# Scratch of q and k in two parts a row instead of three, and the stacks read in two transfers each

## The chip, the cores and the metric

The kernel runs on one core of one Trainium2 chip. The time is device microseconds of one execution of the whole program on that core; the kernel before took 1964.72 us, the median of three runs (1963.83, 1964.72 and 1965.18 us). TensorE is called PE here, VectorE DVE, ScalarE ACT, GpSimd POOL, and SyncE SP. SP computes nothing: it issues nearly all the transfers, in the order of the program, and waits in that order too.

## The reference: what is computed

The kernel adds three things for 2048 tokens of width 512: the input, an attention block with 32 heads of width 16, and a gated MLP that mixes tokens.

```python
xn = _layernorm(x)
# attention
qkv = (xn @ wqkv).reshape(B, S, 3, H, Dh)        # S 2048, H 32, Dh 16
p = softmax(einsum("bhqd,bhkd->bhqk", q, k) * Dh ** -0.5)
a = einsum("bhqk,bhkd->bhqd", p, v).reshape(B, S, D) @ wo
# gated MLP
z = gelu(einsum("bsd,df->bsf", xn, w_in)); z1 = z[..., :896]
z2 = _layernorm(z[..., 896:])
g = einsum("ts,bsf->btf", w_sp, z2) + b_sp
out = x + a + einsum("bsf,fd->bsd", z1 * g, w_out)
```

## The kernel before

**Numbers in two parts.** Products of float32 values are made from a high part, which TensorE's fast float32 format holds exactly, and a low part, the rest. An ordinary product is three matmuls, high by high, low by high and high by low (`mm3`, L161 to L164). For the scores, where a head is only 16 wide, the three are stacked in the rows of one matmul: a head's stack has KS = 48 rows, three for each of the 16 features. A feature's three rows hold high, low, high on the side of q and high, high, low on the side of k, so that one matmul over 48 rows gives all three products.

**Where the stacks come from.** q and k are made for 8 heads at a time (m = 0 to 3) and for 512 tokens at a time (g = 0 to 3), with feature and head across the 128 partitions (`qk_group`, L287). `qk_split` (L305) makes the two parts in a buffer `qkhl`, 128 partitions x 2 x 512, of which there are three (`hilo`, L146): ACT writes the high part, then DVE (m = 0) or POOL (m = 1 to 3) writes the low part. `qk_store` (L278) stores them to the scratch `qscr[m]` or `kscr[m]` in HBM, [128, 3, 2048]: one transfer of 512 KB for both parts and one of 256 KB that stores the high part a second time. The buffer is free for the next split when both have landed. `load_stacks` (L598) reads a head's 48 rows from there into the SBUF tiles `qst` and `kst`, where they lie in partitions 0 to 47 for the first head of a pair and 64 to 111 for the second: for pair 0 in blocks of 512 tokens, in the prologue, and for each later pair in four transfers of 48 rows of 8 KB.

**The order of the work.** The program is written out once, and each engine runs its share of it in that order. A prologue normalises x, makes q and k of the first 8 heads, all of v, and the stacks of pair 0. Then a loop runs over 16 pairs of heads x 4 blocks of queries x 16 tiles of keys. A tile of scores is two matmuls (`st`, L903), one exp on ACT, and the product with v (`o`, L877). The largest score of each row is found 27 tiles ahead: the same scores are made the other way round (`mx`, L630), DVE reduces them (`mm`, L638), and the results go through HBM (`mscr`) into rows 48 and 49 of the stack `qst`. The score tiles and the maxima share three PSUM buffers. A planner fills the rest of TensorE's time with the other matmuls, a few in each half step of the loop: `qk` of the remaining heads, then the MLP, then the product with `wo`. Transfers that need not go at once are put off by some half steps (`later`, L125; in the loop `store` puts a store off by one, L134), and the weights that the filler needs are fetched and split on POOL by `prepare` (L191) in the same manner. The planner decides all this when the program is written, from estimates; on the chip the engines then only wait for each other by semaphores. A transfer's completion is told by one of eight semaphores in turn, so that each transfer also waits for the one eight before it.

**What the change touches.** The scratch tiles (L80 and L81), `qk_store`, `qk_split`, and `load_stacks`. In the order of SP lie around them the reloads of the normalised input (`xnT`), the row maxima (`mscr`), the chunks of the attention output (`escr`), and the weights (`w_`, `wsp_`).

Of the kernel before, what the change touches and what calls it, by code (L numbers as in the profile page):

```python
# [8 lines left out]
F32 = mybir.dt.float32  # L9
F32R = mybir.dt.float32r  # L10
AF = mybir.ActivationFunctionType
# [5 lines left out]
P = 128  # L17
S = 2048
D = 512
H = 32  # L20
DH = 16
# [6 lines left out]
KS = 3 * DH  # L28
# [11 lines left out]
def fused_block(ctx, tc, x, wqkv, wo, w_in, w_spT, b_sp, w_out, out):  # L40
    nc = tc.nc
    cp = ctx.enter_context(tc.tile_pool(name="const", bufs=1))
    dr = ctx.enter_context(tc.tile_pool(name="scratch", bufs=1, space=DRAM))
# [11 lines left out]
    def act(out, in_, func, n, **kw):  # L55
        load["A"] += 0.16 + n / 1400.0
        return nc.scalar.activation(out, in_, func, **kw)  # L57

    def dve(n, rate=1):
        load["D"] += 0.065 + n / (960.0 * rate)  # L60
        return nc.vector
# [15 lines left out]
    qst = [cp.tile([P, S], F32R, name=f"qst{a}") for a in range(2)]  # L77
    kst = [cp.tile([P, S], F32R, name=f"kst{a}") for a in range(2)]

    qscr = [dr.tile([P, 3, S], F32, name=f"qscr{m}") for m in range(4)]  # L80
    kscr = [dr.tile([P, 3, S], F32, name=f"kscr{m}") for m in range(4)]  # L81
    xscr = [[dr.tile([P, 2, 512], F32, name=f"xscr{g}_{c}") for c in range(ND)] for g in range(NG)]
    z2scr = dr.tile([P, NF, 2, NT, P], F32, name="z2scr")
    z1scr = [dr.tile([P, NG, 512], F32, name=f"z1scr{f}") for f in range(NF)]
# [12 lines left out]
    def raw(t):  # L97
        return t.bitcast(F32) if t.dtype == F32R else t

    def move(dst, src):  # L100
        nc.sync.dma_start(raw(dst), raw(src))
# [10 lines left out]
    def clock():  # L112
        return HALF * now[0]

    def gps(us):
        pool[0] = max(pool[0], clock()) + us
        return nc.gpsimd

    def pool_done():
        t = pool[0]  # L120
        yield
        while clock() < t:
            yield

    def later(k, fn, *args):  # L125
        late.append((now[0] + k, fn, args))
# [19 lines left out]
    def hilo(nm):  # L146
        return big.tile([P, 2, 512], F32R, tag="hilo", name=nm, bufs=3)
# [127 lines left out]
                one(c)  # L275


    def qk_store(scr, order, hl, sl, first=False):  # L278
        put = move if first else store
        r = 1 if order[0] == order[1] else 0  # L280
        put(scr[:, r:r + 2, sl], hl)
        put(scr[:, 2 - 2 * r, sl], hl[:, 0, :])

    def qk_weights(m, a):
        return f"wqk{m}_{a}", wqkv[:, a * D + m * P: a * D + (m + 1) * P], D, ND

    def qk_group(m, g, w, tags=("d",)):  # L287
        for a in range(2):
            if now[0] < -2 and m:
                tags = ("d", "o")  # L290
            acc = dpsum(f"qk{m}_{a}_{g}", tags[a % len(tags)], ND)
            for c in range(ND):
                t = xnT[g, c]
                mm3(acc, w[a][:, 0, c * P:(c + 1) * P], w[a][:, 1, c * P:(c + 1) * P], t[:, 0, :], t[:, 1, :], c == 0, c == ND - 1)
                yield 650 + 0.5 * (c == ND - 1)
            if m == 0:
                run(qk_split(m, g, a, acc))
                yield 0
                continue
            raw_ = t512(f"qr{m}_{a}_{g}")  # L300
            act(raw_, acc, AF.Copy, 512)
            side.append(qk_split(m, g, a, raw_))
            yield 0

    def qk_split(m, g, a, src):  # L305
        hl = hilo(f"qkhl{m}_{a}_{g}")
        act(hl[:, 0, :], src, AF.Copy, 512)
        yield
        if m:
            gps(1.3).tensor_sub(hl[:, 1, :], src, hl[:, 0, :].bitcast(F32))  # L310
            yield from pool_done()
        else:
            dve(512).tensor_sub(hl[:, 1, :], src, hl[:, 0, :].bitcast(F32))
        qk_store((qscr, kscr)[a][m], ((0, 1, 0), (0, 0, 1))[a], hl, slice(g * 512, (g + 1) * 512), m == 0)
        yield

    def qk_prepare():
# [280 lines left out]
    def load_stacks(p, cols=slice(0, S)):  # L598
        m, r = p // 4, (p % 4) * 2
        q, k = qst[p % 2], kst[p % 2]  # L600
        sl = [slice((r + j) * DH, (r + j + 1) * DH) for j in range(2)]
        for j in range(2):
            for i, (t, scr) in enumerate(((q, qscr), (k, kscr))):
                args = t[64 * j:64 * j + KS, cols], scr[m][sl[j], :, cols]
                if p and 2 * j + i:
                    later(2 * j + i, move, *args)
                else:
                    move(*args)

# [203 lines left out]
    with tc.manual_schedule(engines=engines):  # L815
# [6 lines left out]
        for c in range(ND):  # L822
            t = (qst, kst)[c // 2][1].rearrange("p (b a f) -> p b a f", b=2, a=2)[:, c % 2]
# [12 lines left out]
        for g in range(NG):  # L836
            for y in qk_group(0, g, w0, ("d", "o")):
                if y == 0 and g == 0:
                    next(norm, 0)
            load_stacks(0, slice(g * 512, (g + 1) * 512))  # L840
            if g == NG - 2:
                for a in range(2):
                    wq[1, a] = begin(*qk_weights(1, a))
            if g == NG - 1:
                for a in range(2):
                    wq[1, a] = end(wq[1, a])
            for t in range(4 * g, 4 * g + 4):
                next(norm, 0)
                if t % 4 == 2:
                    if g + 1 < NG:  # L850
                        turn_x(g + 1)
                    if g + 2 < NG:
                        norm = norm_x(g + 2)
                v_tile(t, wv)
# [50 lines left out]
        order = [(p, c, kt) for p in range(NP) for c in range(NG) for kt in range(NT)]  # L905
# [37 lines left out]
        for half in range(-2 * LEAD // 3, 2 * (N // 3 + 4)):  # L943
# [5 lines left out]
            for n in ns:  # L949
                if n == 16:  # L950
                    init_rows(1)
                if n % 64 == 14 and n // 64 + 1 < NP:
                    load_stacks(n // 64 + 1)
# [99 lines left out]
```

## Time and profile before

| | |
|---|---|
| median of three runs | 1964.72 us |
| the profiled execution: time, span | 1965.23 us, 1963.1 us |
| PE busy | 1933.9 us, 99% of the span |
| DVE, ACT, POOL busy | 1372.9, 1231.7, 720.9 us |
| granted TensorE clock, mean | 0.997 |
| transfers of the SP queue | 282.08 MB, 49.4% of the 16 DMA engines' time |
| HBM written | 101.97 MB |

The profile tells for each engine when it was busy, and for each idle stretch what ended it. A wait is written "engine line <- who: us in total, times, longest". The chain is the work that ended last, followed back from the end, so a step that is not in it costs nothing. A stage of the span is read from a table by windows: the busy time of each engine in that stretch, the granted clock, the share of time in which the DMA engines were busy, and the GB/s moved.

### The profile page before, as it was taken

To read this page: it belongs to the slowest core of one execution; us is meant where nothing else is said; L and a number is where in the kernel's file an instruction comes from. 1 tells how busy PE (TensorE), PEld (TensorE's weight loads), DVE (VectorE), ACT (ScalarE), POOL (GpSimd) and SP (SyncE) were. 2 spreads that over 40 slices of the span, in tenths; PEclk is the share of its full clock that TensorE was granted. 3 is DMA by queue.
4 is the path that set the end of the run, shared out by engine and by line. 5 is a ranking of instruction groups with operands and counts; after the bars stand their busy time and mean duration, and the time that the engine had idled before them with its cause. 6 is when DMAs were issued, how large, how long until landed. Compare 5 with 4: busy or idle time off the path is not lost.

```text
span 1963.1 us, 32545 instructions
## 1 busy us (share of the span) xinstructions
PE 1933.9 (99%) x12544; PEld 1047.0 (53%) x12544; DVE 1372.9 (70%) x1562; ACT 1231.7 (63%) x1402; POOL 720.9 (37%) x787
## 2 busy tenths in 40 slices
PE   7999999999999999999999999999999999999998
PEld 6765555555555555555555555555555555555543
DVE  5256777777777677777777777777777777777872
ACT  4336778888777665656666665665566655556664
POOL 2234368789776931026122531017112300002100
PEclk9999999999999999999999999999999999999999
DMA  9586444363535645365545744346364645355323
GB/s 327 204 292 200 139 107 122 108 176 111 154 117 159 187 123 140 91 162 159 151 138 154 211 129 125 108 126 204 105 163 135 176 142 145 106 152 154 105 73 113
DMA packets 234195, 294.20 MB, mean 150 GB/s; under 512 B 34536, under 2 KB 134520, under 8 KB 231160
## 3 DMA queue, kind: packets, MB, share of 16 engines
q1 hardware_dynamic: 229816, 282.08, 49.4%
q0 software_dynamic: 4224, 10.04, 1.4%
q8 instruction: 99, 1.62, 0.3%
q14 instruction: 56, 0.46, 0.1%
HBM read 190.09 MB, written 101.97 MB: 149 GB/s over the span
## 4 chain that ended last, share of the span: by engine, by line
PE 91%; DVE 3%; POOL 2%; DMA 2%; ACT 1%; issue 1%; SPq 0%; DVEq 0%; POOLq 0%; ACTq 0%
PE o L877 23%; PE mx L630 15%; PE st L903 15%; PE sp L162 7%; PE sp L164 5%; PE sp L163 5%; PE mo L162 2%; PE z1p L162 2%; PE qk L162 1%; DVE mm L638 1%; PE mo L163 1%; PE mo L164 1%; PE z2p L162 1%; PE z1p L164 1%; PE z1p L163 1%; PE qk L163 1%
## 5 line engine op out<-in xcount | busy, mean ns | idle before, releaser
L638 DVE TENSOR_REDUCE mm<-mx 128x2 f32<-128x1024 f32 x1024 | 1221.5, 1222 | 501.3 <-PE mx L630 497.2
L57 ACT ACTIVATE pf<-st 128x1024 f32<-128x1024 f32 x1024 | 1028.7, 1025 | 621.9 <-PE st L903 597.2
L877 PE MATMUL o<-pf,vall 128*32 128x512 f32 (+1 forms) x5120 | 511.0, 513 | 0.0
L630 PE MATMUL mx<-kst,qst 48*128 48x512 f32 x2048 | 446.9, 434 | 3.1 <-DVE mm L638 2.0
L903 PE MATMUL st<-qst,kst 50*128 50x512 f32 x2048 | 445.6, 432 | 1.5 <-DVE mm L638 1.4
L630 PEld LDWEIGHTS mx<-kst,qst 48*128 48x128 f32 x2048 | 192.0, 185 | 268.7 <-ACT pf L57 168.6
L903 PEld LDWEIGHTS st<-qst,kst 50*128 50x128 f32 x2048 | 193.3, 185 | 164.0 <-issue 85.7
L877 PEld LDWEIGHTS o<-pf,vall 128*32 128x32 f32 x5120 | 131.4, 109 | 233.7 <-issue 211.7
L162 PE MATMUL sp<-wsp,zs 128*128 128x512 f32 x448 | 193.8, 433 | 0.3 <-DVE z1i L549 0.2
L556 POOL TENSOR_TENSOR z1i<-z1i,hhl 128x512 f32<-128x512 f32 x28 | 36.0, 1286 | 425.9 <-DVE z1i L549 422.4
L164 PE MATMUL sp<-wsp,zs 128*128 128x512 f32 x448 | 175.9, 393 | 0.0
L163 PE MATMUL sp<-wsp,zs 128*128 128x512 f32 x448 | 175.9, 393 | 0.0
L162 PEld LDWEIGHTS sp<-wsp,zs 128*128 128x128 f32 x448 | 83.9, 187 | 68.9 <-issue 52.1
L164 PEld LDWEIGHTS sp<-wsp,zs 128*128 128x128 f32 x448 | 84.1, 188 | 19.3
L163 PEld LDWEIGHTS sp<-wsp,zs 128*128 128x128 f32 x448 | 84.4, 188 | 12.2
L187 POOL CAST wo<-wo0r 128x512 fp32r<-128x512 f32 x1 | 0.6, 611 | 191.4 <-DMA wo0r<-in_wo 191.4
L310 POOL TENSOR_TENSOR qkhl<-qr,qkhl 128x512 fp32r<-128x512 f32 x24 | 30.9, 1289 | 78.9 <-ACT qkhl L57 78.8
L162 PE MATMUL z2p<-w,xt 128*128 128x448 f32 x128 | 51.3, 401 | 0.0
L162 PE MATMUL mo<-wout,hp 128*128 128x512 f32 x112 | 48.5, 433 | 0.6 <-DVE xr L593 0.4
L691 POOL TENSOR_TENSOR ob<-ob 128x512 f32<-128x512 f32 (+1 forms) x16 | 20.6, 1288 | 77.0 <-DMA ob<-rscr 54.5
L164 PE MATMUL z2p<-w,xt 128*128 128x448 f32 x128 | 46.9, 366 | 0.0
L163 PE MATMUL z2p<-w,xt 128*128 128x448 f32 x128 | 46.8, 365 | 0.0
(378 smaller groups left out, 1974.8 us busy)
## 6 DMA issues: line engine op xcount, KB each, us to landing
zs<-z2scr SPq DMA_DIRECT2D x112, 512.0 KB
escr<-e SPq DMA_DIRECT2D x60, 256.0 KB
hscr<-hhl SPq DMA_DIRECT2D x28, 512.0 KB
qst<-qscr SPq DMA_DIRECT2D x30, 384.0 KB
kst<-kscr SPq DMA_DIRECT2D x30, 384.0 KB
xscr<-xnT POOLq DMA_DIRECT2D x16, 512.0 KB, 6.0
qscr<-qkhl SPq DMA_DIRECT2D x16, 512.0 KB
kscr<-qkhl SPq DMA_DIRECT2D x16, 512.0 KB
```

What stands on the lines that cost most here:

```text
L57: return nc.scalar.activation(out, in_, func, **kw)
L162: nc.tensor.matmul(acc, lh, rh, start=first, stop=False)
L163: nc.tensor.matmul(acc, ll, rh, start=False, stop=False)
L164: nc.tensor.matmul(acc, lh, rl, start=False, stop=last)
L187: gps(0.6).tensor_copy(t[:, 0, :n], rw[:, :n])
L310: gps(1.3).tensor_sub(hl[:, 1, :], src, hl[:, 0, :].bitcast(F32))
L556: gps(1.3).tensor_add(z1, z1, hl[:, 1, :].bitcast(F32))
L630: nc.tensor.matmul(acc[:, j, :], qst[p % 2][rows, tt * P:(tt + 1) * P], kst[p % 2][rows, kc * 512:(kc + 1) * 512], start=True, stop=True)
L638: dve(1024).tensor_reduce(mmax[i // 16][:, :, t, kc], mstep.pop(i), AX.X, ALU.max)
L691: gps(1.3).tensor_mul(both[rows, 0, :], both[rows, 0, :], both[rows, 2, :])
L877: nc.tensor.matmul(acc[cols:cols + VW, a:a + w], vpack(kt - 1 + r, 2 * p + j), pf[:, j * 512 + a:j * 512 + a + w], start=(kt == 1 and a == ...
L903: nc.tensor.matmul(st[:, j, :], kst[p % 2][rows, kt * P:(kt + 1) * P], qst[p % 2][rows, c * 512:(c + 1) * 512], start=True, stop=True)
```

## The change

The scratch keeps two parts a feature instead of three: high, low for q, and low, high for k. `qk_split` writes the parts of k in the other order in the buffer, and one transfer of 512 KB stores them; the second store goes. `load_stacks` reads a head's 48 rows in two transfers: 32 rows of both parts, which lie in HBM without a gap, and the 16 rows of the high part again, every second row of the scratch. A feature's three rows are no longer neighbours in the stack, but q and k still meet as high by low, low by high and high by high, only in another order of the rows. The program of PE, DVE, ACT and POOL is the same instruction for instruction; SP's has 32 stores fewer and 76 reads more.

```diff
-    qscr = [dr.tile([P, 3, S], F32, name=f"qscr{m}") for m in range(4)]
-    kscr = [dr.tile([P, 3, S], F32, name=f"kscr{m}") for m in range(4)]
+    qscr = [dr.tile([P, 2, S], F32, name=f"qscr{m}") for m in range(4)]
+    kscr = [dr.tile([P, 2, S], F32, name=f"kscr{m}") for m in range(4)]
...
-    def qk_store(scr, order, hl, sl, first=False):
-        put = move if first else store
-        r = 1 if order[0] == order[1] else 0
-        put(scr[:, r:r + 2, sl], hl)
-        put(scr[:, 2 - 2 * r, sl], hl[:, 0, :])
...
-        act(hl[:, 0, :], src, AF.Copy, 512)
+        act(hl[:, a, :], src, AF.Copy, 512)
...
-            gps(1.3).tensor_sub(hl[:, 1, :], src, hl[:, 0, :].bitcast(F32))
+            gps(1.3).tensor_sub(hl[:, 1 - a, :], src, hl[:, a, :].bitcast(F32))
...
-            dve(512).tensor_sub(hl[:, 1, :], src, hl[:, 0, :].bitcast(F32))
-        qk_store((qscr, kscr)[a][m], ((0, 1, 0), (0, 0, 1))[a], hl, slice(g * 512, (g + 1) * 512), m == 0)
+            dve(512).tensor_sub(hl[:, 1 - a, :], src, hl[:, a, :].bitcast(F32))
+        (store if m else move)((qscr, kscr)[a][m][:, :, g * 512:(g + 1) * 512], hl)
...
-                args = t[64 * j:64 * j + KS, cols], scr[m][sl[j], :, cols]
-                if p and 2 * j + i:
-                    later(2 * j + i, move, *args)
-                else:
-                    move(*args)
+                two = t[64 * j:64 * j + 2 * DH, cols], scr[m][sl[j], :, cols]
+                one = t[64 * j + 2 * DH:64 * j + KS, cols], scr[m][sl[j], i, cols]
+                for args in (two, one):
+                    if p and 2 * j + i:
+                        later(2 * j + i, move, *args)
+                    else:
+                        move(*args)
```

## The prediction

> **What bounds the kernel.** I read the page first (share of each engine), then a table by windows (where TensorE, PE, is not busy), then the waits and the chain in the one stretch that the change can reach. The page:
>
> ```profile
> PE 1933.9 (99%) x12544; PEld 1047.0 (53%) x12544; DVE 1372.9 (70%) x1562; ACT 1231.7 (63%) x1402; POOL 720.9 (37%) x787
> ```
>
> PE sets the time. Its program is the same before and after, so the change can only take idle time of PE away or add some. The windows (us of the stretch, busy PE and PEld, DVE, ACT, POOL, then granted clock, DMA share, GB/s) show where there is any:
>
> ```profile
> 0.00:14.00 14.00, 4.48 (x17) 3.52 (x18) 7.04 (x21) 6.72 (x11) 6.78 (x17) 1.00 1.02 295
> 14.00:88.00 74.00, 72.00 (x338) 58.87 (x337) 27.05 (x58) 30.09 (x53) 14.07 (x24) 1.00 0.76 281
> 88.00:120.00 32.00, 31.12 (x139) 21.46 (x138) 21.30 (x23) 9.68 (x16) 15.97 (x15) 1.00 0.56 196
> 120.00:150.00 30.00, 27.37 (x117) 18.29 (x117) 15.00 (x13) 12.70 (x19) 10.31 (x8) 0.95 0.86 313
> ...
> 200.00:1900.00 1700.00, 1696.20 (x11242) 895.44 (x11238) 1245.46 (x1384) 1105.24 (x1229) 651.48 (x699) 1.00 0.49 139
> 1900.00:1963.00 63.00, 52.73 (x380) 23.45 (x372) 22.23 (x28) 32.04 (x36) 0.92 (x2) 0.95 0.26 89
> ```
>
> Of 29.2 us idle, 9.5 lie before 14 us (x is loaded), 10.3 after 1900 (no q or k is stored or read there), 3.8 are spread over 1700 us. The prologue's 2.0 and the 0.9 after it wait for DVE or ACT by the waits, not for a transfer. What is left is 2.6 us between 120 and 150, where the clock is at 0.95 too. The waits of 125 to 150 us name it:
>
> ```profile
> ACT qkhl L57 <- DMA kscr<-qkhl: 10.9, 3, 7.2
> ...
> PE qk L162 <- ACT qr L57: 1.5, 1, 1.5
> ...
> PE mx L630 <- DVE mm L638: 1.1, 1, 1.1
> ```
>
> and the chain in order of time (start, duration, what) tells how one leads to the other:
>
> ```profile
> 121.73 3.09 DMA kscr<-qkhl
> ...
> 124.98 0.64 ACT qkhl L57
> ...
> 125.69 1.30 POOL qkhl L310
> 126.99 0.37 SPq L101
> ...
> 127.41 8.61 DMA kscr<-qkhl
> ...
> 136.18 0.63 ACT qkhl L57
> 136.81 0.49 ACT qr L57
> ...
> 137.35 0.50 PE qk L162
> ```
>
> ACT stands before a split whose buffer a store of k still holds; that store lands 8.61 us after its issue. Behind it in ACT's queue stands the eviction `qr`, and PE waits 1.55 us for the PSUM buffer that `qr` frees.
>
> **The change, part by part.**
>
> *Stores.* 32 transfers of 256 KB go, 8.4 MB of 101.97 MB written. Between 121.3 us, where the DMA queue is nearly empty (154 GB/s from 121 to 123), and the landing at 136.0, three pairs of stores (768 KB each) and four reloads of `xnT` (512 KB each) must pass: 4.46 MB. The windows show 376 to 409 GB/s in the full parts of it. Three second stores fewer are 0.79 MB, at 390 GB/s 2.0 us. The splits ahead of it wait for stores too (ACT idle 2.52, 2.89 and 1.24 us), so each starts somewhat sooner; I count none of that. `qkhl` then starts at about 134.2, `qr` is done 1.13 us later, at 135.3, and PE is ready for it at 135.8: the wait of 1.55 us goes, with 0.5 us to spare. What is late next is PE itself. Bounds: 0 (the queue fills up again) and 1.55. I take **-1.55 us**.
>
> *The second wait*, 1.08 us before `mx` at 146.0, ends with the DVE reduction of the maxima tile before, which began 0.02 us after PE had made it. It moves with PE and stays: 0.
>
> *SP.* A store issue takes 0.44 to 0.46 us (medians of `kscr`, `qscr`), a read 0.42. The new store has the shape of the `oscr` stores, 0.57. Net: 76 x 0.42 - 32 x 0.45 + 32 x 0.12 = +21 us of SP time in 1963. SP's waits say that it comes early: it waits 237.3 us for ACT `e`, 210.8 for DVE `ms`, 201.9 for PE `sp`. In the prologue a block has two stores fewer and four reads more, +0.9 us; behind these reads stand the weights `wqk` (issue 84.2, needed at 97.0), and the last block of `kst` itself (issue 83.7, needed about 94.7). Both have over 5 us to spare: 0. A read also waits for the transfer eight places before it, and the eight are now smaller and nearer; of the three largest waits of SP none is of that kind, and nobody waits for SP on the path: 0.
>
> *Reads.* The first matmuls on a stack now wait for up to four transfers, not two. Pair 1 is read from 167 us on and first used at about 210, over 40 us later; what is queued behind such a matmul is all of PE, so without that cover each lateness would count in full, 15 times. The reads of later pairs keep the same place: 0. The bytes are the same, but not the way in: the DMA engines are full while stacks are read, at less than half the rate of other transfers.
>
> ```profile
> 168.00:172.00 4.00, 4.00 (x34) 2.44 (x34) 3.06 (x3) 2.13 (x3) 0.00 (x0) 1.00 1.06 407
> 172.00:176.00 4.00, 4.00 (x27) 2.35 (x20) 2.88 (x3) 3.15 (x5) 1.28 (x1) 1.00 1.10 203
> 176.00:180.00 4.00, 4.00 (x25) 1.73 (x24) 1.97 (x2) 2.58 (x4) 0.00 (x0) 1.00 0.99 168
> ```
>
> At 168 GB/s a stack of 384 KB takes 2.3 us, a pair 9.4. So few rows don't keep the whole way into SBUF busy. Whether 32 rows and then 16 take 2.3 us together, or 2.3 us each and so 4.7, no row shows. I take the same time, the nearest row, and price the other below. The Trainium skill, SBUF — State Buffer, section "Door 1: The DMA port swizzle", says that partition p and p + 32 share a port. By it 48 rows put 8 on the fullest port, 32 put 4 and 16 put 4, so the sum would stay the same; with eight neighbours to a port it would double. The measured 168 GB/s fits either.
>
> **Sum.** 1965.23 (profiled execution: span 1963.1 and 2.1 around it) - 1.55 = 1963.7. The median of the runs shown is 0.5 below the profiled execution, so the forecast is **1963.2 us**, 0.08% faster; about 0.2% (3.9 us) is what a measurement of this kernel can tell from no change.
>
> **Rivals.**
>
> *The clock too.* After the second wait PE ran at about half clock for a while:
>
> ```profile
> 147.00:149.00 2.00, 2.00 (x5) 1.61 (x6) 1.90 (x2) 1.54 (x2) 1.28 (x1) 0.52 0.32 122
> 149.00:151.00 2.00, 2.00 (x12) 0.89 (x10) 0.13 (x1) 0.37 (x1) 0.01 (x1) 0.63 0.54 206
> ```
>
> That cost 2 x 0.48 + 2 x 0.37 = 1.7 us. If the wait at 137 us helped to bring it on, it goes with it: 1961.5. If DVE's wait shrinks as well (at most 1.1), 1960.4. Against it: the drop follows the second wait directly, and that one stays. The Trainium skill, TensorE: Matmul & The Clock Gate, section "Part 1: The HAM clock gate", lets the clock fall after an idle window of some 3.4 us; here 1.08 and 1.55 us of idling, ten apart, were followed by it, so the trace doesn't bear the rule out as it stands.
>
> *Nothing gained.* The reloads of `xnT`, 2 MB of the 4.46, still keep the store until 136: 1964.7. For it: they are the larger part. Against: the bytes taken away are 2.0 us by the measured rate, and 1.5 are enough.
>
> *Slower: stack reads that take twice as long.* Then each pair fills the DMA engines for 9.4 us more. The place is 1079 to 1092 us: the stacks are issued from 1079.0 to 1083.3, and the weights `wsp` of the next block right behind, from 1090.4. POOL already waits 1.4 and 4.8 us there for `wsp_1r` and `wsp_2r`, and PE's weight load 0.4 for `wsp_3r`, so that there is next to no slack. At most 9.4 - 1.55: 1972.6. It decides from 5.5 us of stall on, that is, when a read of a stack takes 1.4 us longer than now. At 169.5 and 637.8, where weights follow stacks too, PE needs them far later (at 221.9 and 678.5). For it: the half rate. Against: the number of bytes is the same, and the reads before left no wait on PE.
>
> **How the numbers follow.** Forecast as told 0.60; nothing gained or up to 3 us lost by small waits 0.15; the clock too 0.15, of which 0.08 beyond 0.2%, with all of it at 1960.4; slow reads 0.10, all beyond 0.2% slower. The range 1960.4 to 1967.5 takes in the first three; its upper end is nothing gained and 2.8 us of a partial stall by the reads. Chances: faster 0.08, slower 0.12 (slow reads and 0.02 of small waits that add up), the rest, 0.80, within 0.2%.
>
> **What would show it.** After: no wait of PE `qk` for ACT `qr` near 136 us, ACT's waits for `kscr` and `qscr` (16 us in all) shrunk to some 6; stretches of stack reads still near 168 GB/s and no longer than 10 us; HBM written 93.6 MB. Wrong if PE waits at a `sp` or `mx` matmul for DMA or POOL, if stack reads run at 100 GB/s or less, or if the half-clock stretches change in number.

## The result and the profile after

The changed kernel takes **1970.62 us** (median of 13 runs, 1968.85 to 1976.2); the kernel before, run beside it, 1965.68 (median of 13, 1963.83 to 1968.49). The ratio is **1.0028**, 95% interval 1.0021 to 1.0036: slower by more than the 0.2% that can be told from no change. The forecast was 1963.2, and its range ended at 1967.5. The profiled execution took 1969.16 us with a span of 1967.4, 4.3 more than before, at a clock of 0.998. HBM written is 93.58 MB, as forecast.

The stretch that the forecast was about did what it should. These are the waits of 125 to 150 us in the changed kernel (us in total, times, longest); PE's 1.5 us at `qk` for ACT `qr` are gone, and the wait at `mx` has stayed:

```profile
ACT qkhl L57 <- DMA kscr<-qkhl: 8.1, 3, 5.4
...
PE mx L627 <- DVE mm L635: 1.1, 1, 1.1
```

The windows (PE busy, PEld, DVE, ACT, POOL, clock, DMA share, GB/s) say where the time came from instead:

```profile
120.00:150.00 30.00, 28.92 (x132) 19.33 (x134) 17.13 (x15) 13.91 (x21) 10.28 (x8) 1.00 0.69 246
...
200.00:1900.00 1700.00, 1692.35 (x11208) 893.09 (x11200) 1241.86 (x1380) 1101.78 (x1226) 650.74 (x698) 1.00 0.49 139
```

Between 120 and 150 us PE is idle 1.1 us instead of 2.6, at full clock instead of 0.95. Between 200 and 1900 us, where the forecast counted nothing, it is idle 7.65 us instead of 3.80. PE's waits over the whole span name two groups that were small before (1.4 us in 5 waits, 0.4 the longest, and 1.2 us in 6, 0.2 the longest):

```profile
PE st L900 <- DVE mm L635: 4.0, 7, 1.3
PE mx L627 <- ACT pf L57: 3.5, 8, 1.2
```

The order of the 12544 matmuls is the same in both kernels, so each can be set against its twin. The changed kernel's PE starts 1.57 us later at 20 us (the start varies from run to run, see the end), gains 1.54 us at 137 us and 1.5 us at 147 to 151, where the half-clock stretch is missing, and then loses in **four steps**: 1.67 us at 198.7 (tile `st31`), 1.63 at 753.6 (`st340`), 1.50 at 1449.6 (`mx761`), 1.24 at 1790.0 (`mx953`), 6.04 us together. (Read over other stretches before and behind it a single step comes out up to 0.3 us different; the sum hardly moves.) Between these places the two run alike. The first step, in order of time (start, duration, engine, line, and in brackets the idle time and its releaser):

```profile
196.42 0.51 PE L900 MATMUL st<-qst,kst 50*128 50x512 f32 x2
...
196.89 0.50 PE L627 MATMUL mx<-kst,qst 48*128 48x512 f32 x2
...
197.43 1.23 DVE L635 TENSOR_REDUCE mm<-mx 128x2 f32<-128x1024 f32 x1 [0.59 <-PE mx L627]
...
198.71 0.50 PE L900 MATMUL st<-qst,kst 50*128 50x512 f32 x2 [1.32 <-DVE mm L635]
```

PE makes the maxima tile `mx57` at 196.89, DVE reduces it from 197.43, and the next score tile, `st31`, which needs nothing of that result, starts in the moment in which DVE is done. The same three tiles in the kernel before stand 0.3 us apart, without a wait:

```profile
197.93 0.50 PE L903 MATMUL st<-qst,kst 50*128 50x512 f32 x2
198.27 0.40 PE L630 MATMUL mx<-kst,qst 48*128 48x512 f32 x2
198.51 0.40 PE L903 MATMUL st<-qst,kst 50*128 50x512 f32 x2
```

A wait without a need for the data is a wait for the place: `st31` has been given the PSUM buffer of `mx57`. The three buffers of `spsum` (L153), which score tiles and maxima share, are not taken strictly in turn. Which of them a tile gets is settled when the program is built, by an estimate of when each comes free; apart from the halves of `qkhl` that the splits of k write, only SP's list differs between the two kernels, so that list must enter the estimate. Read from the two built programs: of 2072 tiles the kernel before departs from "the buffer of three tiles ago" at 24 (12 times two tiles ago and, for the next tile, four), the changed kernel at 54 (19 such pairs, and four times the sequence 2, 1, 5, 4). **The four tiles one back are exactly the four steps.** So "the same instruction for instruction", as the change was described, holds for the order and the form of what PE, DVE, ACT and POOL do; where the tiles lie, and so whom PE waits for, is not the same.

### The profile page after: what moved, and what is told of

Its sections match the earlier page's. It is cut to its first block, busy times and chain, and to the rows that moved or that the text cites. A ratio compares the mean times of both kernels' runs of the same rounds, so it can differ in the third digit from the quotient of the medians.

```text
span 1967.4 us, 32603 instructions
## 1 busy us (share of the span) xinstructions
PE 1934.8 (98%) x12544; PEld 1046.6 (53%) x12544; DVE 1373.2 (70%) x1562; ACT 1232.0 (63%) x1402; POOL 721.6 (37%) x787
## 3 DMA queue, kind: packets, MB, share of 16 engines
HBM read 190.09 MB, written 93.58 MB: 144 GB/s over the span
## 4 chain that ended last, share of the span: by engine, by line
PE 90%; POOL 3%; DVE 3%; DMA 2%; ACT 1%; issue 1%; SPq 0%; DVEq 0%; POOLq 0%; ACTq 0%
PE o L874 22%; PE mx L627 15%; PE st L900 15%; PE sp L162 7%; PE sp L164 5%; PE sp L163 5%; PE mo L162 2%; PE qk L162 2%; PE z1p L162 2%; DVE mm L635 2%; PE qk L163 1%; PE qk L164 1%; PE mo L163 1%; PE mo L164 1%; PE z1p L164 1%; PE z1p L163 1%
```

## Experiments

Theory A: the buffers one back are the loss, and the change in itself is worth what was forecast. The rivals: the reads in two transfers or SP's longer list delay PE, and the buffers only go along with it; or every departure from rotation costs alike; or it is other tiles that have moved, since by the built programs some tiles in SBUF lie elsewhere too (65 of `zs` and 46 of `wsp` among them). In all kernels below, the buffers are fixed by hand:

```diff
+    slot = []
...
-        return ps.tile([P, 2, 512], F32, tag="s", name=nm, bufs=3)
+        i = len(slot)
+        slot.append(i if i < 3 else slot[i - BACK.get(i, 3)])
+        return ps.tile([P, 2, 512], F32, tag=f"s{slot[i]}", name=nm, bufs=1)
```

`BACK` says for single tiles how many tiles back the buffer is taken from. Empty, it is strict rotation.

**The buffers exchanged.** `new_oldbuf` is the changed kernel with the table of the kernel before, `old_newbuf` the kernel before with the table of the changed one:

```diff
+BACK = {46: 2, 47: 4, 50: 2, 51: 4, 251: 2, 252: 4, 347: 2, 348: 4, 374: 2, 375: 4, 407: 2, 408: 4, 1369: 2, 1370: 4, 1405: 2, 1406: 4, 1657: 2, 1658: 4, 1753: 2, 1754: 4, 1849: 2, 1850: 4, 1945: 2, 1946: 4}
```

```diff
+BACK = {46: 2, 47: 4, 50: 2, 51: 4, 104: 2, 105: 1, 106: 5, 107: 4, 218: 2, 219: 4, 251: 2, 252: 4, 347: 2, 348: 4, 350: 2, 351: 4, 374: 2, 375: 4, 407: 2, 408: 4, 614: 2, 615: 4, 722: 2, 723: 1, 724: 5, 725: 4, 1001: 2, 1002: 4, 1003: 2, 1004: 4, 1369: 2, 1370: 4, 1405: 2, 1406: 4, 1511: 2, 1512: 1, 1513: 5, 1514: 4, 1652: 2, 1653: 4, 1753: 2, 1754: 4, 1849: 2, 1850: 4, 1874: 2, 1875: 4, 1876: 2, 1877: 4, 1895: 2, 1896: 1, 1897: 5, 1898: 4, 1945: 2, 1946: 4}
```

> The changed kernel, with the PSUM buffers of the score and maxima tiles given out as in the kernel before (a list says how many tiles back the buffer was last used; three, but for 24 tiles). Theory A: the loss is the four tiles that took the buffer of the tile just ahead of them (about 1.5 us each, 6.0 in all); without them the change is worth what the stretch at 137 us gave, 1.5 us, and up to 1.7 more where the clock stays up: 1.5 to 3 us under the kernel before measured beside it, and no wait of PE over 1.1 us between 150 and 1900 us. Theory B, the rival of the prediction: the reads in two parts are slow or late; then the loss stays, 4 to 6 us over the kernel before.

> The kernel before, stores and reads as they were, with the buffers given out as in the changed kernel (54 tiles off the three-back rotation, four of them one back). Theory A: 6 us over the kernel before, with four new waits of PE of 1.2 to 1.3 us at the score tiles 31 and 340 and the maxima tiles 761 and 953, and the wait of 1.55 us near 137 us still there. Theory B: the same time as the kernel before.

`new_oldbuf`: 1964.32 us, 0.9990 of the kernel before (0.9982 to 0.9999). Its PE waits are back at the old sizes:

```profile
PE st L904 <- DVE mm L639: 1.4, 5, 0.4
...
PE mx L631 <- ACT pf L58: 1.1, 6, 0.2
```

`old_newbuf`: 1973.99 us, 1.0045 (1.0033 to 1.0058). It has the waits of the changed kernel, and at 137 us that of the kernel before:

```profile
PE st L907 <- DVE mm L642: 4.1, 7, 1.3
PE mx L634 <- ACT pf L58: 3.5, 8, 1.2
...
PE qk L166 <- ACT qr L58: 1.2, 1, 1.2
```

That is 2 us more than expected: against the kernel before, the four steps are 6.1 us (1.65, 1.44, 1.66, 1.37), PE starts 2.4 us later at `v` in this profile, and a half-clock stretch of 6.8 us behind the first step costs 3.1; the half-clock stretch at 147 us, which is missing here, gives 1.5 back. The loss goes with the buffers, not with the transfers: theory A. In `new_oldbuf` every tile outside these three buffers lies as in the changed kernel, so the tiles that moved in SBUF are not the cause either.

**Strict rotation.** `new_rot` is the changed kernel, `old_rot` the kernel before, each with `BACK = {}`.

> The changed kernel with the three buffers given out in strict rotation, each tile three back. Theory A: at most 1 us from the changed kernel with the old buffers, since a buffer two or four back costs little: 1.5 to 4 us under the kernel before. Theory B: 4 to 6 us over it.

> The kernel before with the three buffers in strict rotation. Theory A: within 1.5 us of the kernel before; if the 1.6 us that PE stands idle between 400 and 500 us come from the tiles two or four back, up to 2 us under it. Theory B says nothing on it: the same time.

`new_rot` 1963.67 us, 0.9985 (0.9977 to 0.9994); `old_rot` 1965.38, 0.9999 (0.9990 to 1.0008). So the change without its accident is 0.0014 faster by the ratios (2.8 us; their intervals leave some 0.4 to 5 open), 1.7 us by the medians, and `new_rot` is faster than both kernels.

**Only the four.** `rot_four` departs from rotation at these places alone:

```diff
+BACK = {n + d: b for n in (104, 722, 1511, 1895) for d, b in enumerate((2, 1, 5, 4))}
```

> The changed kernel with strict rotation except at the four places where the changed kernel took the buffer of the tile just ahead (`st31`, `st340`, `mx761`, `mx953`). Theory A: these four carry nearly all of the loss, 6.0 us by the profile of the changed kernel, so 1.0010 to 1.0025 times the kernel before (strict rotation 0.9985 and 5 to 8 us). Rival from the run with 200 places two back (0.1 us each): the other 19 pairs of places carry a part, some 2 us, so 1.5 to 2 us less than the changed kernel's 1.0028.

1970.28 us, 1.0029 (1.0019 to 1.0039), against 1.0028 for the changed kernel. The four carry the loss; this measurement can't see whether the other departures add to it, and the upper end of what theory A was given (1.0025) was a little low.

**Forty places one back, and two hundred two back.**

```diff
+BACK = {104 + 44 * n + d: b for n in range(40) for d, b in enumerate((2, 1, 5, 4))}
```

```diff
+BACK = {104 + 9 * n + d: b for n in range(200) for d, b in enumerate((2, 4))}
```

> The changed kernel with the three score buffers in strict rotation, but at 40 places, 44 tiles apart, a tile takes the buffer of the tile just ahead of it. Theory A (such a place makes PE wait until the tile ahead is made and reduced or exponentiated): 1.24 to 1.67 us each, as at the four places of the changed kernel, so 50 to 67 us above strict rotation, which was 0.9985 of the kernel before: some 2015 to 2030 us, and 40 waits of PE `st` for DVE `mm` of 1.3 us each among PE's waits. Theory B (the four stalls were something else, such as late transfers at these places, and the buffers only a companion): no more than a few us, under 1970.

> The changed kernel with strict rotation, but at 200 places a tile takes the buffer of the tile two places back instead of three, and the next that of four back. Theory A: a place two back has the slack of a whole tile and costs next to nothing, as at the 24 places of the kernel before: within 2 us of strict rotation, 0.998 to 0.9995 of the kernel before. Theory B (every departure from rotation costs, and the 30 added places of the changed kernel share its loss): 6 us / 30 = 0.2 us each, 40 us in all, some 2005 us.

`one_back40`: 2033.84 us, 1.0346 (1.0332 to 1.0360), 72 us above strict rotation (0.9985 of 1964.77, the kernel before beside it), 1.8 us a place. PE's waits:

```profile
PE st L904 <- DVE mm L639: 36.8, 31, 1.3
PE mx L631 <- DVE mm L639: 15.0, 14, 1.1
```

With the 5 waits and 1.9 us that `new_rot` has there taken off, these are 40 waits and 49.9 us, 1.25 each. Behind eight of them PE ran for 3.4 us at half clock, 1.7 us each, 14 us; the other 8 us are 0.2 a place. That is more than the 67 us expected at most, by these eight. `two_back200`: 1982.80 us, 1.0086 (1.0073 to 1.0100), 20 us above rotation, 0.1 us a place: neither the 0 of theory A nor the 0.2 of its rival. Hardly any of it appears as a wait; the profile counts it as busy time of PE, 1951.1 us against 1935.8 in `new_rot`. Two back is nearly enough cover, one back is none. By that the 12 pairs of the kernel before would cost some 1.2 us, and the 7 that the changed kernel added 0.7, an estimate too small for `old_rot` (0.9999) to bear out or refute.

**The reads alone.** `reads_only` is `old_rot` (three parts, two stores) with a stack read in 32 and 16 rows:

```diff
-                args = t[64 * j:64 * j + KS, cols], scr[m][sl[j], :, cols]
...
+                two = t[64 * j:64 * j + 2 * DH, cols], scr[m][sl[j], 0:2, cols]
+                one = t[64 * j + 2 * DH:64 * j + KS, cols], scr[m][sl[j], 2, cols]
```

> The kernel before with strict rotation and the change's reads alone: the scratch keeps three parts, both stores stay, and a stack's 48 rows are read in 32 rows and 16 rows. Theory A (the reads cost nothing): as strict rotation alone, 0.9999 of the kernel before with an interval of 0.1% to either side; PE's wait of `qk` for ACT `qr` near 137 us is still there. Rival (split reads are slow and hold up what is queued behind them): 2 us or more slower, and PE waits for weights or stacks behind the reads.

1965.71 us, 1.0003 (0.9995 to 1.0012), against 0.9999 for `old_rot`: 0.8 us by the ratios, each known to 0.0009. The wait at 137 us is there, and one at a weight is new beside it:

```profile
PE qk L166 <- ACT qr L58: 1.9, 1, 1.9
...
PE sp L168 <- POOL wsp L192: 0.6, 1, 0.6
```

So the reads cost between nothing and some 3 us by these intervals, and the stores bring the gain: from `reads_only` to `new_rot` it is 0.0018, 3.5 us (some 1 to 6). In the profiles part of it lies far from 137 us: near 1578 us PE waits 1.4 us at a product `mo` in `old_rot` and 1.5 us in `reads_only`, there for the load of `hp`, and in `new_rot` it doesn't.

**The reads doubled, two probes that failed.** `reads_twice` reads each stack a second time at once, `reads_later` 14 half steps later:

```diff
-                for args in (two, one):
+                for args in (two, one, two, one) if p else (two, one):
```

```diff
+                    if p:
+                        later(14 + 2 * (2 * j + i), move, *args)
```

> The changed kernel with strict rotation, in which each stack of pairs 1 to 15 is read twice, by the same two transfers one after the other (the second leaves the same data): 120 transfers and 23.6 MB more. Theory A (the reads have slack on all places but perhaps one): within 2 us of strict rotation, 0.9975 to 0.9995 of the kernel before, or up to 5 us more if the weights `wsp` behind the stacks of 1079 to 1083 us come late. Rival (the reads are on the path): 0.5 to 2 us for each of 15 pairs, 7 to 30 us slower.

> The changed kernel with strict rotation, in which each stack of pairs 1 to 15 is read a second time, 14 half steps and more behind the first, when the first has landed, so that SP should not have to stand and wait as in the run where both reads followed at once (284 us of SP's waits were for `kst<-kscr` and `qst<-qscr`). The 23.6 MB more fill the DMA engines for another 9.4 us a pair, as in the prediction's rival of slow reads. Theory A (that run was slow because SP waited, not because of the bytes): under 5 us above strict rotation, below 1.001. Rival (the transfers themselves hold up the row maxima `mscr` or the weights): 1 to 6 us a pair, 15 to 90 us.

2076.19 us, 1.0564 (1.0550 to 1.0578), and 2181.84 us, 1.1106 (1.1091 to 1.1121). Neither measured the transfers. In the first, SP stood before each second read until the first had landed, and the row maxima were issued behind it, too late; in the second, the second read had to wait until PE had read the stack, and PE waited for it in turn. SP's waits and one of PE's in `reads_twice`, then one of PE's in `reads_later`:

```profile
SPq L102 <- DMA kst<-kscr: 146.8, 52, 6.5
...
SPq L102 <- DMA qst<-qscr: 137.3, 48, 6.2
```

```profile
PE st L904 <- DMA qst<-mscr: 43.8, 18, 12.2
```

```profile
PE mx L633 <- DMA kst<-kscr: 90.6, 27, 9.5
```

A second write to the same rows brings its own waits. What twice the bytes cost without these is left open. The first probe shows one thing all the same: what suffers first when SP is held up at the stacks is the transfer of the row maxima, not the weights `wsp` that the forecast named.

## Why the prediction was wrong

**The step that failed** stands in its first part: "Its program is the same before and after, so the change can only take idle time of PE away or add some". What was the same is the order and the form of the instructions. The buffers that their tiles lie in were not compared, and the sum has no term for them. That term is about +6 us: 6.04 in the profile of the changed kernel, and 0.0044 of the time by the runs (8.6 us, `rot_four` less `new_rot`; each ratio is known to about 0.0010). In the profile of `rot_four` a half-clock stretch follows one of the four stalls, in that of the changed kernel none; the mean granted clock of the changed kernel's 13 executions was 0.995 to 0.998, so the term need not be the same in each. None of the rivals had this mechanism.

**Stores, -1.55 us: right.** The wait is gone, 1.54 us at that place, and with fitting buffers the kernel is faster by 1.3 us by the medians (`new_oldbuf`; 0.2 to 3.5 by the interval of its ratio) or 1.7 us (`new_rot` against `old_rot`). ACT's waits for `kscr` and `qscr` shrank by less than thought, from 16.3 us to 12.0 and not to some 6, but the place that mattered was cleared.

**The second wait, 0: right.** 1.1 us before and after, and in `new_oldbuf`. But this row already had the mechanism in it that the sum lacks. The tile that waits, `mx28`, doesn't need the reduction that ends its wait; it is one of the 24 tiles of the kernel before (46 in its table, two back) and lies in the buffer of `mx27`, which DVE is reducing. In `new_rot`, three back, PE stands 0.67 us there and not 1.08.

**SP, 0: not refuted.** `new_oldbuf` has all its added issues and loses nothing that can be measured. (The +0.9 us a block in the prologue comes to 1.0 by the prices given beside it, which changes nothing.)

**Reads, 0: nearly.** At the place that the rival of slow reads named, the reads did slow down. All work stands there 2 us later in the changed kernel, so the same two stretches of work are, in the kernel before and then in the changed one:

```profile
1087.00:1089.00 2.00, 2.00 (x10) 1.58 (x9) 2.00 (x2) 1.03 (x1) 1.10 (x1) 1.00 1.07 187
1089.00:1091.00 2.00, 2.00 (x16) 0.67 (x15) 0.95 (x2) 1.02 (x2) 0.00 (x0) 1.00 1.04 260
```

```profile
1089.00:1091.00 2.00, 2.00 (x11) 1.53 (x9) 2.00 (x2) 1.03 (x1) 1.13 (x1) 1.00 1.09 148
1091.00:1093.00 2.00, 2.00 (x17) 0.73 (x15) 0.95 (x2) 0.96 (x2) 0.00 (x0) 1.00 0.89 98
```

PE is busy throughout in both. By the records of its packets the pair of stacks there took 16.2 us, from its first packet to the end of its last, instead of 12.6; 3.6 more is under the 5.5 from which the rival was to decide. Over all 15 pairs the mean, with other transfers in between, is 13.2 us against 12.8, so 32 and 16 rows cost nearly what 48 cost, not twice. (The Trainium skill, SBUF — State Buffer, section "Door 1: The DMA port swizzle", from which the same sum was worked out, agrees with that.) Two of the signs by which the forecast was to be known as wrong did come, reads at 98 GB/s and a half-clock stretch fewer, and neither is where the time went; pairs that take longer than 10 us were there before the change (10.3 to 19.3 us).

**The clock too: open.** The stretch at 147 us is missing after, but it is there in `new_oldbuf`, where the wait at 137 is gone too, so it doesn't hang on that wait; whether it comes hangs, by the last section, on where the stall before it happens to fall, so the 1.5 us that the changed kernel's profile gains there are luck. In `old_rot`, and likewise in `reads_only`, a half-clock stretch follows the wait at 137 itself, and a second one begins at 150 or 151 us:

```profile
138.00:140.00 2.00, 1.45 (x6) 1.17 (x7) 0.10 (x1) 1.24 (x4) 1.31 (x2) 0.93 0.94 362
140.00:142.00 2.00, 2.00 (x6) 1.54 (x5) 0.00 (x0) 1.00 (x2) 1.34 (x2) 0.50 0.91 338
```

In `new_rot` both are missing, with the wait. That may be why the stores bring 3.5 us there and not 1.6; one profile of each doesn't settle it, the less as those of `old_rot` and `reads_only` are of the slowest execution of each (1970.44 and 1971.39 us, against medians of 1965.38 and 1965.71).

## What to carry to other kernels

An edit that leaves every engine's instructions and their order alone can still move tiles to other buffers, if a planner deals out the buffers of a pool by its own estimate, so before a forecast compare for each tile whose place it takes and not only the order. A wait for an engine whose result the waiting instruction doesn't need is a wait for a place: look there for the tile that held it last. Where PE is the bound, hand out the buffers in a fixed turn (here worth 0.0043 of the time, 8 us, to the changed kernel), or at least keep tiles that follow each other apart.

## What the runs showed of the hardware

A short stall can halve the clock, and need not. The stall before `mx` near 145 us is the same in the changed kernel as in `new_oldbuf` (PE busy 0.94 and 0.92 of 2 us), but the stretch behind it is not, first in the changed kernel, then in `new_oldbuf`:

```profile
148.00:150.00 2.00, 2.00 (x13) 0.85 (x16) 1.40 (x2) 1.43 (x2) 1.04 (x1) 1.00 0.00 0
```

```profile
148.00:150.00 2.00, 2.00 (x6) 1.16 (x6) 0.72 (x1) 0.37 (x1) 0.81 (x1) 0.50 0.00 0
```

In `one_back40`, of 40 stalls of about 1.1 to 1.3 us eight were followed by one. The records of the clock change in steps of 3.413 us, counted from the first record of each trace, and a stall's place among these steps matters. In the profiles of the ten kernels that read no stack twice, PE stands still for 1.0 us or more 62 times between 30 and 1950 us. Of the 41 stalls that lie within one step, 14 were followed by half clock; of the 21 that lie across the border of two steps, none. The stall near 145 us lies within a step in the kernel before and in `new_oldbuf`, and across a border in the changed kernel. What decides among the 41 stays open, and so does the reason. The Trainium skill, TensorE: Matmul & The Clock Gate, section "Part 1: The HAM clock gate", has windows of that length that run on freely, which agrees; it drops the clock after an idle window, and here 1.1 to 1.3 us of idling were enough.

The start varies too: PE's wait at `v` for DVE `qkhl` near 21 us was 0 to 3.1 us long in these profiles, whatever the kernel. Differences of 1 to 2 us between single profiles mean nothing until the places of the difference are found.
